# Casting q and k in the transfer, and turning them head by head

## The chip, the cores and the metric

The kernel runs on one core of one Trainium2 chip. The metric is the device time of one execution in microseconds (us). The kernel before took 433.94 us, the median of three runs (433.75 to 435.5).

## The reference

The inputs are q, k and v of shape (8 batches, 8 heads, 576 positions, 64), float32, eight global positions, and two weight matrices, 512 x 2048 and 2048 x 512. The attention is a local window of 32 positions to each side, with global rows and columns:

```python
scores = scale * np.matmul(q, k.transpose(0, 1, 3, 2))
mask = np.abs(pos[:, None] - pos[None, :]) <= window
mask = mask | is_global[:, None] | is_global[None, :]
scores = np.where(mask, scores, -1000000000.0)
attn = np.exp(scores - np.max(scores, axis=-1, keepdims=True))
attn = attn / (np.sum(attn, axis=-1, keepdims=True) + 1e-09)
attn_out = np.matmul(attn, v)
x = attn_out.transpose(0, 2, 1, 3).reshape(B * S, H * D)      # 4608 x 512
h = x @ w_in
g = np.maximum(h, 0.0) + np.log1p(np.exp(-np.abs(h)))         # softplus
out = g @ w_out                                               # 4608 x 512, float32
```

## The kernel before

The work is cut twice. Attention is cut into 72 units: a unit is one block of 64 positions of one batch, all eight heads, nine units to a batch. The two dense layers are cut into nine tiles of 512 tokens, that is eight units each, so a tile's borders and a batch's borders don't fall together. The matmuls of the dense layers are bf16, as are the matmuls of attention; scores and exponentials are float32.

For each batch there is a preparation. SP's queue loads k and q in float32 into three staging buffers `qk`, 72 partitions by 4 heads by 512 numbers (`load_qk`: each partition holds eight neighbouring positions of every head). Each half is two DMAs, of 64 and of 8 partitions. A cast (`add_cast`, L444 and L442) rounds it to bf16 and reorders it into `qn` or `kn`, one buffer each, so that the two heads of a pair stand side by side in 128 columns. TensorE transposes these (`tk`, `tq`, L512 and L518): eight transposes of 72 x 128 for each of the four head pairs, of k and of q. The results go to `kx` and `qz` by copies on ACT or DVE (`kev`, `qev`, L402). `pick` (L472) gathers the rows of the global positions out of `qn` and `kn` by 64 small matmuls. v is loaded in five pieces by SP (`load_v`, 256 bytes at a time), cast to `vA`, and a copy of it that is shifted by 64 rows, `vB`, is made by two DMAs from SBUF to SBUF (`shift`, L452 and L453).

A unit then runs as a chain over the engines: scores `s` on TensorE (L625), mask and row maximum on DVE (L631), exponentials `pe` on ACT (L652), row sums `sm` and reciprocals `rs` on DVE (L660 to L662), scaling to `pn` on POOL (L668), and the global columns `gw`, also POOL (L672), a transpose `tp` on TensorE (L678) and its copy `pt`. After four units `rt` (L704) and `xo` (L721, L728) make the attention output, and a copy of it is `xT`, the input of the dense layers. In batch 0 the first eight units take their row sums from ACT.

A tile runs its 64 matmuls `h` (L763), each 16th of them followed by a softplus `g` on ACT (L768), and then its 64 matmuls `o` (L773). The scores of the next tile's units lie among the `h` matmuls, and the exponentials, scaling and transposes among the `o` matmuls. A table load on ACT (L565) marks the step from softplus to the exponentials in each tile.

Each engine works through its queue in order. The order is made when the program is built: every piece of work is a job with a cost per engine, the jobs it depends on, a rank, and the buffers and PSUM banks that it opens or uses. `_Order.run` plays these jobs against a clock and takes, at each step, the one that could start first. A job of kind "DMA" is put on SP's queue; the weights are loaded by POOL's queue, which rounds them to bf16 on the way (`weights_in`, `weights_out`, L803 and L807, four DMAs each). The costs only decide the order and, where a job may run on several engines, which one takes it.

At the start SP loads k, q and v of batch 0. The casts of batch 0 are spread over DVE, ACT and POOL:

```python
            add_cast(b, 1, [["DVE"], ["ACT"], ["DVE"], ["DVE"]])
            add_cast(b, 0, [["DVE"], ["ACT"], ["POOL"], ["DVE"]])
            T["w_in"] = o.add({"POOL": (2400, 18000)}, weights_in, [T["cast", 0, 0][2]], rank=0)
            T["w_out"] = o.add({"POOL": (3000, 30000)}, weights_out, [T["cast", 0, 0][2]], rank=1)
            add_cast(b, 2, [["POOL", "ACT"]] * NT5)
```

All later casts are POOL's. The loads of batch 1 wait for a tiny DMA (`hold`) that reads the last piece of w_in. `blank_q` and `blank_g` clear the buffers of batches 0 and 1 on POOL, `make_band`, `mask_left`, `mask_right`, `mask_global`, `make_places` and `ones_g` build masks and places on DVE.

Of the kernel before, what the change touches and what calls it, by code (L numbers as in the profile page):

```python
# [18 lines left out]
class _Order:  # L19
# [15 lines left out]
    def add(self, cost, emit, deps=(), rank=5, opens=(), uses=(), table=None):  # L35

        job = dict(cost=cost, emit=emit, deps=[d for d in deps if d is not None], rank=rank, opens=list(opens),
                   table=table, n=len(self.jobs), at=None, end=None)
        self.jobs.append(job)
        for pool, key in job["opens"]:  # L40
            self.users.setdefault(key, []).append(job)
        for key in uses:
            self.users.setdefault(key, []).append(job)
        return job
# [30 lines left out]
    def run(self, free):  # L75
# [11 lines left out]
        dma = 0  # L87
        while ready:
            best = None
            for j in ready:  # L90
                t0 = max([d["at"] if d["on"] in j["cost"] and d["on"] in ("PE", "DMA") else d["end"] + self.HOP
# [27 lines left out]
            if e == "DMA":  # L119
                dma = max(dma, t + 1500) + took  # L120
                j["at"], j["end"] = t, dma + 500
            else:
                j["at"], j["end"] = t, t + took
# [14 lines left out]
def kernel(  # L138
# [10 lines left out]
    nc = tc.nc  # L149
# [47 lines left out]
    stage = ctx.enter_context(tc.tile_pool(name="stage", bufs=3))  # L197
# [9 lines left out]
    def load_qk(b, which, half):  # L207

        st = PS["in", b, which, half] = stage.tile([P, HP, QR * D], FP32, tag="qk", name="qk")
        src = SRC[which][b, half * HP:(half + 1) * HP].rearrange("h (q r) d -> q h (r d)", r=QR)  # L210
        for lo, hi in ((0, 64), (64, NQ)):
            nc.sync.dma_start(out=st[lo:hi, :, :], in_=src[lo:hi])

    qn = const([P, QR, H * D], BF16, "qn")
    kn = const([P, QR, H * D], BF16, "kn")
# [44 lines left out]

    mask = const([P, NJ, EXT], BF16, "mask")
# [29 lines left out]
    def mask_left():  # L291
        nc.vector.tensor_copy(mask[:, :, 0:G], band[:, 0:G].unsqueeze(1).to_broadcast([P, NJ, G]))
        nc.vector.memset(mask[:, 0, 0:WIN], NEG)

    def mask_right():
        nc.vector.tensor_copy(mask[:, :, W:EXT], band[:, G:P].unsqueeze(1).to_broadcast([P, NJ, G]))
        nc.vector.memset(mask[:, NJ - 1, EXT - WIN:EXT], NEG)
# [23 lines left out]
    def blank_q(i):  # L321
        for p in range(HP):
            nc.gpsimd.memset(qz[i][0:D, p, :, 1, :].bitcast(I32), 0)
            nc.gpsimd.memset(qz[i][D:P, p, :, 0, :].bitcast(I32), 0)

    def blank_g(i):
        nc.gpsimd.memset(kx[i][:, :, 0, 0:WIN].bitcast(I32), 0)
        nc.gpsimd.memset(kx[i][:, :, NH5 - 1, G - WIN:G].bitcast(I32), 0)
        clear(nc.gpsimd, pg[i][:])
        clear(nc.gpsimd, qg[i][:])  # L330
        clear(nc.gpsimd, lg[i][:])
        clear(nc.gpsimd, gw[i][:])
        nc.gpsimd.memset(vA[i][0:WIN, 0, :].bitcast(I32), 0)
        nc.gpsimd.memset(vA[i][96:P, NT5 - 1, :].bitcast(I32), 0)
        clear(nc.gpsimd, oz[i][:])
# [29 lines left out]
    SLOTS = dict(xT=2, osb=2, st=7, pe=3, pn=4, pt=5, R=2, small=2, gk=2, in_qk=3, in_v=3)  # L365
# [42 lines left out]
    def add_load(b, which, deps):  # L408
        if which < 2:
            parts = [(1700, lambda e, x=x: load_qk(b, which, x)) for x in range(2)]  # L410
        else:
            parts = [(1160, lambda e, x=x: load_v(b, x)) for x in range(NT5)]
        T["load", b, which] = [o.add({"DMA": (100 if which == 2 else 700, took)}, emit, deps, rank=0,
                                     opens=[("in_v" if which == 2 else "in_qk", ("in", b, which, x))])
                               for x, (took, emit) in enumerate(parts)]

    def add_cast(b, which, engines):
        n_parts = len(engines)
        early = []
        if which < 2:  # L420
            early += [T.get(("t" + "qk"[which], b - 1, p)) for p in range(HP)]
            early += [T.get(("pick", b - 1, x)) for x in range(2)]
        else:
            early += [T.get(("val", n4)) for n4 in range(NU)
                      if any((n4 * 4 + u) // NJ == b - 2 for u in range(4))]
            early += [T.get(("ov", b - 2)), T.get(("shift", b - 2)), T["blank_g", min(b, 1)]]
        T["cast", b, which] = []
        for n, who in enumerate(engines):
            loads = T["load", b, which]

            def emit(e, n=n):
                if which < 2:
                    to = (qn, kn)[which][:, :, n * P:(n + 1) * P].rearrange("q r (h d) -> q r h d", h=2)
                    at = PS["in", b, which, n // 2][:, n % 2 * 2:n % 2 * 2 + 2, :]
                    at = at.rearrange("q h (r d) -> q r h d", r=QR)
                else:
                    to, at = vA[b % 2][:, n, :], PS["in", b, 2, n][:, :]
                rows = [slice(0, NQ)] if which < 2 else {0: [slice(32, 64), slice(64, P)],
                                                         NT5 - 1: [slice(0, 96)]}.get(n, [slice(0, P)])
                for r in rows:  # L440
                    if e == "ACT":
                        nc.scalar.copy(to[r], at[r])  # L442
                    else:
                        (nc.gpsimd if e == "POOL" else nc.vector).tensor_copy(to[r], at[r])  # L444
            w = QR * P if which < 2 else H * D
            cost = {"POOL": (110 + .862 * w, 110 + .862 * w), "ACT": act(w, False), "DVE": dve(w, False)}
            T["cast", b, which].append(o.add({e: cost[e] for e in who}, emit,
                                             [loads[n * len(loads) // n_parts]] + early, rank=6 if b else 0,
                                             uses=[("in", b, which, n * len(loads) // n_parts)]))
        if which == 2:  # L450
            def shift(e):
                nc.sync.dma_start(out=vB[b % 2][0:64, :, :], in_=vA[b % 2][64:P, 0:NT5 - 1, :])  # L452
                nc.sync.dma_start(out=vB[b % 2][64:P, :, :], in_=vA[b % 2][0:64, 1:NT5, :])  # L453
            T["shift", b] = o.add({"DMA": (100, 3000)}, shift, T["cast", b, 2] + early, rank=0)

    def add_prep(b, gate, rank):
# [4 lines left out]
        if b < 2:  # L461
            blanks = {x: [T["blank_" + x, b]] for x in "qg"}
        XN = (qn, kn)

        def pick(e, ws):
# [3 lines left out]
            for w in ws:  # L469
                for r in range(QR):  # L470
                    for p in range(HP):
                        nc.tensor.matmul(out=PS["pick", b][p * 32:(p + 1) * 32, w, 0:P], lhsT=pick_w[0:NQ, r, :],  # L472
                                         rhs=XN[w][0:NQ, r, p * P:(p + 1) * P], start=(r == 0), stop=(r == QR - 1))
# [20 lines left out]
        for n, ws in enumerate(steps):  # L494
            T["pick", b, n] = o.add({"PE": (460 * len(ws) + 190, 460 * len(ws) + 300)}, lambda e, ws=ws: pick(e, ws),
                                    [x for w in ws for x in T["cast", b, w]] + [T.get(("pick", b, n - 1))], rank=4,
# [11 lines left out]
        for p in range(HP):  # L508
            def tk(e, p=p):
                ps = PS["tk", b, p] = psum(("tk", b, p), [P, QR, NQ], BF16)  # L510
                for r in range(QR):
                    nc.tensor.transpose(out=ps[:, r, :], in_=kn[0:NQ, r, p * P:(p + 1) * P],  # L512
                                        identity=ident_b[0:NQ, 0:NQ])

            def tq(e, p=p):
                ps = PS["tq", b, p] = psum(("tq", b, p), [P, QR, NQ], BF16)
                for r in range(QR):
                    nc.tensor.transpose(out=ps[:, r, :], in_=qn[0:NQ, r, p * P:(p + 1) * P],  # L518
                                        identity=ident_b[0:NQ, 0:NQ])
# [13 lines left out]
            T["tk", b, p] = o.add(mm(QR, NQ), tk, [T["cast", b, 1][p], *gate], rank=rank, opens=[("tk", ("tk", b, p))])  # L533
            T["kev", b, p] = o.add({"ACT": (640, 740), "DVE": (870, 950)}, kev, [T["tk", b, p], *late, *blanks["g"]],
                                   rank=3, uses=[("tk", b, p)])
            T["tq", b, p] = o.add(mm(QR, NQ), tq, [T["cast", b, 0][p], *gate], rank=rank, opens=[("tq", ("tq", b, p))])
# [77 lines left out]
    def add_scores(n, gate, rank):  # L614
# [19 lines left out]
        for x in range(2):  # L634
# [5 lines left out]
            T["top", n, x] = o.add({"DVE": (440, 600)}, lambda e, x=x: top(e, x), [T["sc", n, x], *T["mask", 0]], rank=4,  # L640
# [172 lines left out]
    for w in (1, 0, 2):  # L813
        add_load(0, w, T["load", 0, 0] if w == 2 else [])
    T["band"] = setup(make_band, {"DVE": (1500, 1600)}, rank=2)
    T["mask", 0] = [setup(fn, {"DVE": (cost, cost + 100)}, [T["band"]], 2)
                 for fn, cost in ((mask_left, 850), (mask_right, 850), (mask_global, 1400))]
    T["places"] = setup(make_places, {"DVE": (1300, 1400)}, T["mask", 0], 3)
    T["select"] = setup(select_rows, {"DVE": (500, 600)}, [T["places"]], 3)
    for i in range(2):  # L820
        T["blank_q", i] = setup(lambda i=i: blank_q(i), pool(2750), [T["load", 0, 2][-1]] if i else [], 1 + 5 * i)
        T["blank_g", i] = setup(lambda i=i: blank_g(i), pool(2400), [T["blank_q", i]], 1 + 5 * i)

    def add_ones(i, after):
        T["ones_g", i] = setup(lambda i=i: ones_g(i), {"DVE": (1500, 1600)}, [T["blank_g", i], T["places"], T["select"], *after],
                               1 + 5 * i)
# [12 lines left out]
    def make_batch(b, gate, rank):  # L839
# [3 lines left out]
        if b == 1:  # L843
            add_ones(1, [T["su", NJ - 3]])

            def hold(e):
                nc.sync.dma_start(out=held[0:1, :], in_=w_in_t[KD - 1][0:1, 0:16])
            T["hold"] = o.add({"DMA": (100, 100)}, hold, [T["w_in"], T["shift", 0]], rank=0)
        for w in (1, 0, 2):
            if b:  # L850
                add_load(b, w, [T["hold"]] if b == 1 else [T["cast", b - 1, w][-1]])
# [61 lines left out]
```

## Time and profile before

| what | value |
|---|---|
| median of three runs | 433.94 us (433.75 to 435.5) |
| the profiled execution | 437.42 us, of which the span of the profile is 435.7 |
| PE busy | 363.8 us, 83% of the span |
| PE weight loads | 203.3 us, 47% |
| ACT busy | 290.7 us, 67% |
| DVE busy | 257.0 us, 59% |
| POOL busy | 189.5 us, 44% |
| bytes moved by the DMA engines | 46.92 MB, of which 41.96 on SP's queue and 4.19 on POOL's |
| matmuls h, o | 134.8 and 135.1 us busy |

The profile is of one execution, and its times are counted from the start of its span. PE is TensorE's matmuls and PEld its weight loads, which overlap. "Busy" counts the time in which an instruction of the engine runs, and matmuls are pipelined, so that the busy time of one (0.2 us for a small one) is longer than the distance to the next. In a timeline, the time in brackets is the idle time of the engine before the row and what ended it. Idle time of an engine counts only where others wait for it. The DMA share is the mean busy share of 16 DMA engines, and goes over 1 where packets overlap. The trace also has a record of each DMA packet: its start, its queue and its size as written.

### The profile page before, as it was taken

How to read it: one execution, taken by the hardware profiler on the slowest of the kernel's cores; microseconds unless marked ns; L12 is line 12 of the kernel's file. 1: busy time of each engine (PE TensorE's matmuls, PEld its weight loads, DVE VectorE, ACT ScalarE, POOL GpSimd, SP SyncE). 2: the span in 40 equal slices, each digit the busy share in tenths (PEclk: the TensorE clock that was granted, in tenths of full speed). 3: DMA queues.
4: the chain of work that ended last, by engine and by line, in shares of the span. 5: the costliest groups of instructions: out<-in, count | busy, mean ns of one | idle time of the engine just before them, and what ended most of it. 6: DMA issues, size and time to landing. Idle time of an engine off the chain costs nothing.

```text
span 435.7 us, 12000 instructions
## 1 busy us (share of the span) xinstructions
PE 363.8 (83%) x4583; PEld 203.3 (47%) x4640; DVE 257.0 (59%) x1104; ACT 290.7 (67%) x717; POOL 189.5 (44%) x301
## 2 busy tenths in 40 slices
PE   0540769998999898998999899889988997998996
PEld 0420645555444644464446444645464444544442
DVE  3592746497539843695579447944894495547001
ACT  2471746887568863887588758876887785696730
POOL 6435786459215741376138513780461062036000
PEclk9999969999999998999999999999999999999999
DMA  7899999982961397129812881083114011002001
GB/s 153 136 207 225 220 163 177 181 175 84 220 126 48 99 190 140 48 70 197 162 48 71 199 159 50 26 170 69 50 46 98 0 50 52 0 24 74 3 24 72
DMA packets 56873, 46.92 MB, mean 108 GB/s; under 512 B 39408, under 2 KB 41456, under 8 KB 56816
## 3 DMA queue, kind: packets, MB, share of 16 engines
q1 hardware_dynamic: 54128, 41.96, 45.4%
q0 software_dynamic: 2688, 4.19, 5.3%
q8 instruction: 36, 0.59, 0.6%
q14 instruction: 21, 0.17, 0.1%
HBM read 36.71 MB, written 9.44 MB: 106 GB/s over the span
## 4 chain that ended last, share of the span: by engine, by line
PE 34%; DVE 21%; POOL 14%; DMA 13%; ACT 8%; issue 7%; SPq 2%; DVEq 0%; POOLq 0%; ACTq 0%
PE h L763 20%; DMA qk<-in_q_dram 7%; DVE sm L660 6%; PE o L773 6%; DMA v<-in_v_dram 5%; POOL kn L444 4%; POOL pn L668 3%; POOL qn L444 3%; DVE rs L662 3%; POOL vA L444 2%; DVE oz L596 2%; ACT L565 2%; DVE rs L661 2%; PE s L625 2%; DVE pt L402 2%
## 5 line engine op out<-in xcount | busy, mean ns | idle before, releaser
L763 PE MATMUL h<-xT,win 128*128 128x512 bf16 x552 | 134.8, 383 | 10.9 <-ACT xT L402 6.5
L668 POOL TENSOR_TENSOR pn<-pe,rs 128x512 bf16<-128x512 f32 x72 | 74.8, 1039 | 146.6 <-DVE rs L662 140.9
L773 PE MATMUL o<-wout,g 128*128 128x512 bf16 x543 | 135.1, 379 | 2.0 <-issue 0.8
L768 ACT ACTIVATE g<-h 128x512 bf16<-128x512 f32 x144 | 85.1, 597 | 58.4 <-PE h L763 58.2
L652 ACT ACTIVATE pe<-st,nb 128x136 f32<-128x136 f32 x288 | 94.3, 400 | 19.7 <-POOL gw L672 18.0
L631 DVE CUSTOM_DVE_ANT_0 st<-s,mask 128x136 f32<-128x136 f32 x288 | 69.7, 294 | 44.3 <-PE s L625 43.8
L763 PEld LDWEIGHTS <-win 128*128 128x128 bf16 x576 | 54.3, 99 | 62.6 <-issue 12.3
L773 PEld LDWEIGHTS <-g 128*128 128x128 bf16 x576 | 52.5, 98 | 48.0
L660 DVE TENSOR_REDUCE sm<-pe 128x4 f32<-128x544 f32 x64 | 45.5, 711 | 5.2 <-ACT pe L652 5.0
L444 POOL CAST qn<-qk 72x1024 bf16<-72x1024 f32 x29 | 30.1, 1066 | 36.4 <-DMA qk<-in_q_dram 35.0
L678 PE MATMUL tp<-ident_b,pn 128*128 128x128 bf16 x288 | 29.7, 230 | 18.9 <-POOL pn L668 15.1
L444 POOL CAST vA<-v 128x512 bf16<-128x512 f32 (+3 forms) x45 | 27.0, 608 | 26.5 <-DMA v<-in_v_dram 25.1
L678 PEld LDWEIGHTS <-pn 128*128 128x128 bf16 x288 | 17.9, 101 | 42.1 <-POOL pn L668 40.9
L625 PE MATMUL s<-kx,qz 128*128 128x136 bf16 x288 | 32.3, 235 | 2.7 <-DVE qz L402 2.3
L625 PEld LDWEIGHTS <-qz 128*128 128x128 bf16 x288 | 23.1, 103 | 18.7 <-DVE qz L402 2.6
L402 DVE COPY qz<-tq 64x576 bf16<-64x576 bf16 x32 | 23.5, 748 | 12.5 <-PE tq L518 8.9
L444 POOL CAST kn<-qk 72x1024 bf16<-72x1024 f32 x28 | 28.3, 1036 | 0.9 <-PE pick L472 0.7
L402 DVE COPY pt<-tp 128x512 bf16<-128x512 bf16 x51 | 21.3, 419 | 9.7 <-PE tp L678 9.0
L402 ACT COPY qz<-tq 64x576 bf16<-64x576 bf16 x32 | 20.3, 636 | 8.2 <-DVE qz L402 7.5
L402 ACT COPY kx<-tk 128x32 bf16<-128x32 bf16 (+1 forms) x75 | 19.1, 330 | 7.8 <-PE tk L512 7.7
L512 PE MATMUL tk<-ident_b,kn 72*128 72x72 bf16 x256 | 14.9, 209 | 11.1 <-ACT kn L442 9.8
L402 DVE COPY osb<-o 128x512 f32<-128x512 f32 x12 | 8.2, 686 | 26.4 <-PE o L773 26.4
(126 smaller groups left out, 447.2 us busy)
## 6 DMA issues: line engine op xcount, KB each, us to landing
out_dram<-osb SPq DMA_DIRECT2D x36, 256.0 KB
qk<-in_k_dram SPq DMA_DIRECT2D x16, 512.0 KB
qk<-in_q_dram SPq DMA_DIRECT2D x16, 512.0 KB
v<-in_v_dram SPq DMA_DIRECT2D x24, 256.0 KB
vB<-vA SPq DMA_DIRECT2D x16, 256.0 KB
v<-in_v_dram SPq DMA_DIRECT2D x16, 192.0 KB
win<-in_moe_w_in_dram POOLq DMA_DIRECT2D x4, 512.0 KB, 9.0
wout<-in_moe_w_out_dram POOLq DMA_DIRECT2D x4, 512.0 KB, 19.4
```

The source lines that it names most:

```text
L402: (nc.scalar.copy if e == "ACT" else nc.vector.tensor_copy)(out, in_)
L444: (nc.gpsimd if e == "POOL" else nc.vector).tensor_copy(to[r], at[r])
L512: nc.tensor.transpose(out=ps[:, r, :], in_=kn[0:NQ, r, p * P:(p + 1) * P], identity=ident_b[0:NQ, 0:NQ])
L625: nc.tensor.matmul(out=ps[:, y, :], lhsT=qz[i][:, x * 2 + y, j, :, :], rhs=kf[:, x * 2 + y, j * W:j * W + EXT], start=True, stop=True)
L631: nc.vector.tensor_tensor_reduce(out=PS["st", n][:, p, :], in0=PS["s", n, x][:, y, :], in1=mask[:, j, :], scale=-SCALE, scalar=3.0e38, op0 ...
L652: nc.scalar.activation(out=pe[:, p, 0:EXT], in_=PS["st", n][:, p, :], func=AF.Exp, bias=PS["nb", n][:, p:p + 1], scale=-1.0, **({"accum_ou ...
L660: nc.vector.reduce_sum(out=sm[:], in_=PS["pe", n][:, :, 0:EXT], axis=AX)
L668: nc.gpsimd.tensor_tensor(out=pn[:].rearrange("c p (a s) -> c p a s", a=2), in0=wide[:, :, :, 0:G], in1=rs[:].unsqueeze(2).unsqueeze(3).to ...
L678: nc.tensor.transpose(out=ps[:, p, :], in_=PS["pn", n][:, p, :], identity=ident_b[:])
L763: nc.tensor.matmul(out=h[:, :], lhsT=w_in_t[kd][:, c * P:(c + 1) * P], rhs=PS["xT", m][:, kd, :], start=(kd == 0), stop=(kd == KD - 1))
L768: nc.scalar.activation(out=t[:, :], in_=PS["h", m, c][:, :], func=AF.Softplus)
L773: nc.tensor.matmul(out=PS["o", m, ns][:, :], lhsT=PS["g", m, kf][:, ns * P:(ns + 1) * P], rhs=w_out_t[kf // 4][:, kf % 4, :], start=(kf == ...
```

## The change

q and k are loaded by POOL's queue, one DMA of 72 partitions for all eight heads, which rounds to bf16 on the way. The staging buffers and the casts of q and k go away. `qn` and `kn` become two buffers each, one for even and one for odd batches, and hold the heads one after the other. The transposes therefore work on one head at a time: 16 of 72 x 64 for each head pair in place of 8 of 72 x 128, the even head into the upper 64 partitions of PSUM and the odd one into the lower. `pick` reads the same rows in the new layout.

At the start POOL issues k and q of batch 0 first, then w_in, then k and q of batch 1, then w_out. v of batch 0 waits for a tiny DMA that reads `qn` of batch 0, and v of batch 1 for one that reads w_in. v has five staging buffers in place of three. From batch 2 on all loads wait for the last cast of the batch before. `blank_q` clears batch 0's buffers on DVE, one side of the mask may be copied by ACT, and the planner has a clock for each DMA queue and other costs. In the built program POOL's queue has, ahead of the first `pn`, the issues of batch 1's k and q and of w_out and all blanks; among the first eight `pn` the five casts of batch 1's v (in six instructions); and in later tiles four of the five casts of v (in five instructions, before: three casts in four) ahead of the eighth `pn`, then the last cast, and the issues of the next k and q. SP's queue has, for each batch, the four output stores of the second half of a tile, the two shifts, and then the five loads of the next v. On PE `pick` stands after 24 matmuls `h` in tiles 1 to 4 (before: after 40 or more).

```diff
-    def load_qk(b, which, half):
-        st = PS["in", b, which, half] = stage.tile([P, HP, QR * D], FP32, tag="qk", name="qk")
-        src = SRC[which][b, half * HP:(half + 1) * HP].rearrange("h (q r) d -> q h (r d)", r=QR)
-        for lo, hi in ((0, 64), (64, NQ)):
-            nc.sync.dma_start(out=st[lo:hi, :, :], in_=src[lo:hi])
-    qn = const([P, QR, H * D], BF16, "qn")
-    kn = const([P, QR, H * D], BF16, "kn")
+    qn = [const([P, H, QR * D], BF16, f"qn{i}") for i in range(2)]
+    kn = [const([P, H, QR * D], BF16, f"kn{i}") for i in range(2)]
+    def load_qk(b, which):
+        nc.gpsimd.dma_start(out=(qn, kn)[which][b % 2][0:NQ, :, :],
+                            in_=SRC[which][b].rearrange("h (q r) d -> q h (r d)", r=QR))
+    for which in (1, 0):
+        load_qk(0, which)
...
+    def blank_q(i, eng):
...
+    blank_q(0, nc.vector)
...
+    def mask_side(e, x):
+        copy(e, mask[:, :, x * W:x * W + G], band[:, x * G:x * G + G].unsqueeze(1).to_broadcast([P, NJ, G]))
...
-                                         rhs=XN[w][0:NQ, r, p * P:(p + 1) * P], start=(r == 0), stop=(r == QR - 1))
+                                         rhs=XN[w][0:NQ, p * 2:p * 2 + 2, r * D:(r + 1) * D],
+                                         start=(r == 0), stop=(r == QR - 1))
...
-                    nc.tensor.transpose(out=ps[:, r, :], in_=kn[0:NQ, r, p * P:(p + 1) * P],
-                                        identity=ident_b[0:NQ, 0:NQ])
+                    for h in range(2):
+                        nc.tensor.transpose(out=ps[h * D:(h + 1) * D, r, :],
+                                            in_=kn[i][0:NQ, p * 2 + h, r * D:(r + 1) * D],
+                                            identity=ident_b[0:NQ, 0:NQ])
...
+    for w in (1, 0):
+        add_load(0, w, [])
+    add_load(0, 2, [hold("v", T["load", 0, 0], qn[0][0:1, 0, 0:16])])
+
+    T["w_in"] = o.add({"POOL": (2400, 0)}, weights_in, [], rank=0, moves=("POOL", 14000))
+    for w in (1, 0):
+        add_load(1, w, [T["w_in"]])
+    T["w_out"] = o.add({"POOL": (3000, 0)}, weights_out, T["load", 1, 0], rank=1, moves=("POOL", 12000))
...
-            T["hold"] = o.add({"DMA": (100, 100)}, hold, [T["w_in"], T["shift", 0]], rank=0)
...
+            add_load(b, 2, [hold("w", [T["w_in"]], w_in_t[KD - 1][0:1, 0:16])])
+        elif b:
             for w in (1, 0, 2):
-                add_cast(b, w, [["POOL"]] * (HP if w < 2 else NT5))
+                add_load(b, w, [T["w_out"], T["cast", b - 1, 2][-1]])
+        add_cast(b, ["POOL"] if b else ["POOL", "ACT"])
```

## The prediction

> **What bounds the kernel now.** I read the page first (busy shares, the chain), then busy time by stretch, then the timelines of POOL, SP and PE. The page:
>
> ```profile
> span 435.7 us, 12000 instructions
> PE 363.8 (83%) x4583; PEld 203.3 (47%) x4640; DVE 257.0 (59%) x1104; ACT 290.7 (67%) x717; POOL 189.5 (44%) x301
> PE   0540769998999898998999899889988997998996
> DMA  7899999982961397129812881083114011002001
> ```
>
> TensorE bounds it, but the first five or six slices are thin on PE and full on DMA. By stretch (us, then busy us and count for PE, PEld, DVE, ACT, POOL; clock, DMA share, GB/s):
>
> ```profile
> 30.00:40.00 10.00, 1.91 (x28) 1.06 (x26) 4.34 (x28) 4.44 (x24) 2.54 (x7) 1.00 1.15 214
> 40.00:50.00 10.00, 4.25 (x35) 3.43 (x36) 6.05 (x44) 5.55 (x29) 8.00 (x20) 1.00 1.17 242
> 128.20:151.80 23.60, 21.35 (x367) 12.61 (x369) 19.48 (x56) 20.07 (x59) 13.47 (x22) 1.00 0.22 66
> 195.00:217.60 22.60, 20.05 (x269) 11.19 (x270) 12.31 (x71) 15.01 (x26) 9.09 (x10) 1.00 0.87 178
> ```
>
> So there are two regimes: a start short of data, then tiles of some 43 us, over 90% PE. The start, in POOL's timeline (start us, us, engine and line, what; in brackets the idle time before and what ended it):
>
> ```profile
> 20.36 2.35 POOL L803 DMA_DIRECT2D win<-in_moe_w_in_dram  x4
> 22.67 3.02 POOL L807 DMA_DIRECT2D wout<-in_moe_w_out_dram  x4
> 37.27 0.61 POOL L444 CAST vA<-v 96x512 bf16<-96x512 f32 x1 [11.58 <-DMA v<-in_v_dram]
> 43.18 1.04 POOL L668 TENSOR_TENSOR pn<-pe,rs 128x512 bf16<-128x512 f32 x1
> 57.78 1.04 POOL L668 TENSOR_TENSOR pn<-pe,rs 128x512 bf16<-128x512 f32 x1 [1.45 <-ACT kx L402]
> ```
>
> POOL issues the weights at 20.36, stands 11.58 us behind the last piece of v, blanks batch 1's buffers, and only at 43.18 scales the first unit; the eighth, which tile 0's w_in matmuls need, at 57.78. In a settled tile, rows of the timelines of POOL, SP and PE:
>
> ```profile
> 193.61 1.03 POOL L668 TENSOR_TENSOR pn<-pe,rs 128x512 bf16<-128x512 f32 x1
> 197.23 0.51 SPq L452 DMA_DIRECT2D vB<-vA  x1
> 199.92 0.40 PE L625 MATMUL s<-kx,qz 128*128 128x136 bf16 x4
> 210.92 0.61 PE L472 MATMUL pick<-qn,pick 72*32 72x128 bf16 x29 [0.36 <-POOL qn L444]
> ```
>
> The gather of global rows (pick) is the only place where PE waits for q: 2.9 us over all later tiles. What pick gathers here was issued by SP as the staging buffers came free, part of it a tile earlier, and cast by POOL.
>
> **Rates from the packet records.** Software queue alone: 203 packets/us of 1 KB written (w_out), 49/us of 4 KB (w_in). When SP's queue has work too, the two alternate one to one: 49 and 50/us at 28-33 us (w_in with v), about 150 and 150 at 34-36 (w_out with v's 256 B), 67 and 62 at 42-43 (w_out with vB's 4 KB). v alone: 400 to 980/us. First packet 2.55 us after an issue (20.36 to 22.9); a reader starts 0.75 us after the last.
>
> **The start, part by part.** k and q are 576 packets each: issued near 0.8, first packet 3.4, both moved by 9-10 and ready by 11, against 17.2 before. The casts vanish. w_in follows in the same queue: 512/49 = 10.5 us, to 20. v waits for q (the hold), starts near 13, and gets 49/us until w_in is through: 350 of 4608 packets. Its second piece, for which POOL's queue waits, lands near 24, its last at 28-29; ACT's queue holds casts of v ahead of the exponentials, so the first of these stays near 32 (29.65 before). POOL then issues k, q of batch 1 and w_out (4.5 us by L803/L807's 0.6-0.75 each), blanks batch 1's buffers (5.4 us by 37.81 to 43.18): first pn near 35, 8 us earlier. That is not kept; what is late next is batch 1's v. k and q run to 35, w_out's 2048 packets at 150/us to 49, and v gets the same 150/us: its pieces land near 39, 46, 51, 52 and 53. POOL's new order has their casts between pn 4 and pn 8, so the eighth pn comes near 54.5, not 57.78: 3.3 us gained. A further 1.0 us of batch-1 transposes leaves the w_in phase. Start: -4.3 us (-9 if v is not held back, 0 if SP issues v 4 us later). The other edits of the setup (DVE blanks batch 0's q and k buffers, ACT copies one side of the mask, the order of masks and ones) are 3 us of DVE and under 1 us of ACT at a time when both stand waiting for q and then v, until 28; I cost them at nothing, and at 3 us if v were early.
>
> **Turning by head.** 8 transposes of 128 columns become 16 of 64. Eight start every 0.26 us (191.62, 191.88, 192.14): 72 columns, 32.5 ns each. Bounds for 16: 0.26 us if two column tiles overlap fully, as four 32-column tiles do (xo L728: four 64-column matmuls per 29 ns); 0.52 us if they don't. Loads may pace them between. I take 0.4, as column tiles do overlap here: 8 x 0.14 = 1.1 us a batch, against 0.3 us of PE slack ahead of the eighth tp. The Trainium skill (TensorEngine Tiling (Array Packing), Restrictions) says that column tiling disables the fast weight load. With the P/1.2 ns that its page TensorE: Matmul & The Clock Gate, LDWEIGHTS (loading the stationary operand), gives a plain load of P columns, an estimate by these pages is 53 ns for each of two tiles side by side, 0.43 us for 16, and 1.4 us a batch where I take 1.1; no run here shows a 64-column load.
>
> **Settled tiles.** POOL loses 8 casts of 1.03 us, all off the path but for pick. One more v cast (0.58) now stands before the eighth pn: 193.61 becomes 194.2. Then gw, the last v cast, and only now the issue of the next k (196.0): the loads no longer run a tile ahead of their cast, so pick waits on the transfer itself. First packet 198.5. SP, released by the same cast, has vB's 128 packets of 4 KB (198.1 to 200.5), then v: k gets 125 packets by 200.5, the rest at 150/us ends at 203.5, q at 207.4, ready at 208.1. PE's new order puts pick after 24 w_in matmuls: 199.92 + 5.04 = 204.96, plus 0.6 to 1.2 of the above. So PE waits 2 to 2.5 us each tile. Behind pick on PE stand 40 w_in matmuls, for which ACT's softplus and then the next softmax wait, so nothing hides it: the tile is 208.1 - 204.96 = 3.1 us longer than with q in time (turning's cost is inside it). Alone on the engines, 1152/203 = 5.7 us, q would be ready at 205.0: no wait.
>
> The skill (DMA: Bandwidth & Descriptors, Why a DMA increments its semaphore by 16 and not by 1) has a rule against the new shape: a DMA spreads over the largest number of engines up to 16 that divides its slowest dimension, which for 72 rows is 12. By it, an estimate, the 9 us of k and q would stretch by up to a third, pick would wait 2.5 us more in five tiles, and the sum would be 451; its exception (some copies from the software queue still spread over all) would leave the sum below. The trace has no 72-row transfer, only SP's 64 and 8 rows.
>
> **Sum.** Periods between exp table loads before (82.50, 128.24, 174.45, 217.63, 260.79, 303.46, 344.85): 45.7, 46.2, 43.2, 43.2, 42.7, 41.4. New for the first four: 43.18 - 0.36 + 3.1 = 45.9, that is +0.2, -0.3, +2.7, +2.7. The fifth has pick later: +1.5; the sixth only the turning: +0.6. Together +7.4. After 1.5 us of pick waits at 165-167 the clock fell to half for 3.4 us (0.92 over 151.8-174.5); I allow one such fall, +1.7 (half of 3.4; that of before is already out of the second period). Total -4.3 + 7.4 + 1.7 = +4.8. The profiled run took 437.42 (span 435.7 plus 1.7 around it), 3.5 over the median of 433.94; added to the run it is 442.2, to the median 438.7, which is the forecast.
>
> **Rivals.** *q and k land before pick* (other side): the first packet is earlier or v yields the engines. It decides when issue to landing is under 10 us (196.0 to 205.9). For it: the 5.7 us alone. Against: the one-to-one rows. Then tiles 1 and 2 lose their old extra (45.7 and 46.2 to 43.6: -4.7), four pay 0.5 for cast and turning (+2), and the start gives -4.3: -7, 427. With batch 1's v unhindered too: 423.
> *Loss without limit in one place*: transposes serial (8 x 0.26 = 2.1 us a tile, partly under the wait) and clock halved in three more tiles: 438.7 + 5 + 2 = 446.
> *Cancelling*: waits of 1 us only: 434.
>
> **How the numbers follow.** Forecast case 0.44 (its own range 434.5 to 443), q in time 0.34, cancelling 0.12, serial 0.10. About 0.5% (2.2 us) is what a measurement tells from no change. Faster: 0.34 and a little of the cancelling case, 0.37; same 0.15; slower 0.48. Range 423 to 447.
>
> **What would show it.** Right: first pn near 35 and eighth near 54; pick waiting 2 us on DMA of q in tiles 1 to 4; 16 transposes in 0.3-0.5 us. Wrong: a k or q transfer under 10 us from issue, or an eighth pn before 50: then faster.

## The result, and the profile after

The changed kernel took 477.0 us (median of four runs, 474.59 to 477.57), the kernel before beside it 434.72 us: a ratio of 1.0945, 95% interval 1.087 to 1.1021. The forecast was 438.7 us with a range of 423 to 447, so the time is 30 us above the range. The profiled run took 477.57 us, its span is 475.9 us, 40.2 us longer than the span before.

The page of the changed kernel:

```profile
span 475.9 us, 12908 instructions
...
PE 384.9 (81%) x5152; PEld 212.1 (45%) x5152; DVE 256.4 (54%) x1109; ACT 290.1 (61%) x716; POOL 141.4 (30%) x249
...
PEclk9999679999699979998799979999799999999999
...
L458 PE MATMUL pick<-qn,pick 72*32 72x128 bf16 x256 | 7.5, 288 | 35.1 <-DMA qn<-in_q_dram 35.1
...
kn<-in_k_dram POOLq DMA_DIRECT2D x8, 576.0 KB, 11.6
qn<-in_q_dram POOLq DMA_DIRECT2D x8, 576.0 KB, 14.8
```

POOL lost 48 us of work (189.5 to 141.4) with the casts of q and k. But PE now stands 35.1 us in front of one instruction, `pick`, and the thing that ends the wait is the transfer of q itself. The clock row has a dip to 6 or 7 about every four slices of 11.9 us, once in each of five tiles, beside the one at the start. One settled tile, by the timelines of POOL, SP and PE (start us, us, engine and line, what, in brackets the idle time before and what ended it):

```profile
103.82 0.88 POOL L213 DMA_DIRECT2D kn<-in_k_dram  x1
104.70 0.80 POOL L213 DMA_DIRECT2D qn<-in_q_dram  x1
...
104.71 0.47 SPq L438 DMA_DIRECT2D vB<-vA  x1
105.27 0.55 SPq L439 DMA_DIRECT2D vB<-vA  x1
105.87 16.08 SPq L205 DMA_DIRECT2D v<-in_v_dram  x5
...
111.90 1.03 PE L754 MATMUL h<-xT,win 128*128 128x512 bf16 x4
121.39 1.04 PE L458 MATMUL pick<-qn,pick 72*32 72x128 bf16 x32 [8.46 <-DMA qn<-in_q_dram]
122.22 1.07 PE L458 MATMUL pick<-kn,pick 72*32 72x128 bf16 x32
123.22 1.89 PE L754 MATMUL h<-xT,win 128*128 128x512 bf16 x4
```

k and q leave POOL at 103.8 and 104.7, just as SP gives out vB and v. PE reaches `pick` at 112.9 and gets q at 121.4. After the wait, four `h` matmuls take 1.89 us; four ran in 1.03 before it. The same tile by stretches (stretch, us, then busy us and count for PE, PEld, DVE, ACT, POOL; granted clock, DMA share, GB/s):

```profile
107.00:123.00 16.00, 7.54 (x100) 4.41 (x98) 2.90 (x24) 5.02 (x8) 0.00 (x0) 0.81 0.99 165
...
123.00:128.00 5.00, 5.00 (x30) 2.17 (x22) 1.82 (x11) 1.57 (x3) 0.00 (x0) 0.58 0.16 37
```

PE works 7.5 of 16 us, and when it may go on it does so at little more than half clock. The table puts the five tiles together. The periods are those between exp table loads (82.20, 136.18, 187.82, 241.94, 293.66, 343.49, 385.01 after). The stretches of half clock are from the trace's record of the granted clock.

| tile | period after, before (us) | forecast of the difference | measured | wait of pick for q | half clock that began in the wait |
|---|---|---|---|---|---|
| 1 | 53.98, 45.74 | +0.2 | +8.2 | 8.46 | 10.24 |
| 2 | 51.64, 46.21 | -0.3 | +5.4 | 6.69 | 6.83 |
| 3 | 54.12, 43.18 | +2.7 | +10.9 | 8.62 | 10.24 |
| 4 | 51.72, 43.16 | +2.7 | +8.6 | 6.79 | 6.83 |
| 5 | 49.83, 42.67 | +1.5 | +7.2 | 4.32 | 6.83 |
| 6 | 41.52, 41.39 | +0.6 | +0.1 | none | none |

The start gave 0.3 us (82.20 against 82.50) where 4.3 were forecast, and what follows the last table load is equal (90.9 us in both). So the whole loss lies in five tiles, and it looks like 34.9 us of waits and the half clock behind them. Each fall of the clock begins inside its wait; 5.8, 4.9, 5.9, 4.9 and 5.6 us of half clock, 27.2 in all, lie behind the waits. The experiments had to show three things: that these waits are the cause and not the work, why the transfer takes so long, and where the forecast gain at the start went.

### The profile page after: what moved, and what is told of

Its sections match the earlier page's. It is cut to its first block, busy times and chain, and to the rows that moved or that the text cites. A ratio compares the mean times of both kernels' runs of the same rounds, so it can differ in the third digit from the quotient of the medians.

```text
span 475.9 us, 12908 instructions
## 1 busy us (share of the span) xinstructions
PE 384.9 (81%) x5152; PEld 212.1 (45%) x5152; DVE 256.4 (54%) x1109; ACT 290.1 (61%) x716; POOL 141.4 (30%) x249
## 4 chain that ended last, share of the span: by engine, by line
PE 41%; DMA 21%; DVE 18%; POOL 8%; ACT 6%; issue 5%; SPq 0%; POOLq 0%; DVEq 0%
PE h L754 22%; DMA qn<-in_q_dram 19%; PE o L764 8%; POOL pn L659 5%; DVE sm L651 5%; PE tp L669 3%; PE s L616 2%; DMA v<-in_v_dram 2%; DVE oz L587 2%; PE pick L458 2%; DVE rs L653 2%; POOL vA L431 2%; DVE st L622 2%; ACT L556 2%; DVE rs L652 1%
## 5 line engine op out<-in xcount | busy, mean ns | idle before, releaser
L754 PE MATMUL h<-xT,win 128*128 128x512 bf16 x576 | 145.0, 395 | 4.6 <-DVE xT L404 2.9
L764 PE MATMUL o<-wout,g 128*128 128x512 bf16 x576 | 140.6, 379 | 0.0
L669 PE MATMUL tp<-ident_b,pn 128*128 128x128 bf16 x288 | 29.9, 229 | 16.5 <-POOL pn L659 16.2
L458 PE MATMUL pick<-qn,pick 72*32 72x128 bf16 x256 | 7.5, 288 | 35.1 <-DMA qn<-in_q_dram 35.1
L616 PE MATMUL s<-kx,qz 128*128 128x136 bf16 x288 | 33.9, 243 | 1.4 <-DVE qz L404 0.8
L616 PEld LDWEIGHTS <-qz 128*128 128x128 bf16 x288 | 24.8, 108 | 19.9 <-issue 4.5
L458 PEld LDWEIGHTS <-pick 72*32 72x32 bf16 x512 | 11.8, 132 | 47.0 <-DMA qn<-in_q_dram 37.4
L404 DVE COPY qz<-tq 64x576 bf16<-64x576 bf16 x34 | 25.4, 751 | 6.7 <-PE tq L508 3.5
L404 DVE CAST gk<-pick 128x256 bf16<-128x256 f32 x6 | 2.5, 424 | 43.8 <-PE pick L458 43.7
L712 PE MATMUL xo<-R,oz 128*32 128x256 bf16 (+3 forms) x384 | 19.5, 258 | 5.5 <-ACT R L404 5.1
L622 DVE DVE_READ_ACCUMULATOR2_ANT nb<- 128x1 f32 x288 | 23.9, 83 | 0.0
## 6 DMA issues: line engine op xcount, KB each, us to landing
qn<-in_q_dram POOLq DMA_DIRECT2D x8, 576.0 KB, 14.8
```

What stands on the lines that cost most here:

```text
L404: (nc.scalar.copy if e == "ACT" else nc.vector.tensor_copy)(out, in_)
L616: nc.tensor.matmul(out=ps[:, y, :], lhsT=qz[i][:, x * 2 + y, j, :, :], rhs=kf[:, x * 2 + y, j * W:j * W + EXT], start=True, stop=True)
L622: nc.vector.tensor_tensor_reduce(out=PS["st", n][:, p, :], in0=PS["s", n, x][:, y, :], in1=mask[:, j, :], scale=-SCALE, scalar=3.0e38, op0 ...
L669: nc.tensor.transpose(out=ps[:, p, :], in_=PS["pn", n][:, p, :], identity=ident_b[:])
L754: nc.tensor.matmul(out=h[:, :], lhsT=w_in_t[kd][:, c * P:(c + 1) * P], rhs=PS["xT", m][:, kd, :], start=(kd == 0), stop=(kd == KD - 1))
L764: nc.tensor.matmul(out=PS["o", m, ns][:, :], lhsT=PS["g", m, kf][:, ns * P:(ns + 1) * P], rhs=w_out_t[kf // 4][:, kf % 4, :], start=(kf == ...
```

## Experiments: is it the wait?

**Loads a tile earlier.** The double buffers allow k and q of a batch to be issued long before the last cast of v of the batch before.

```diff
-                add_load(b, w, [T["w_out"], T["cast", b - 1, 2][-1]])
+                add_load(b, w, [T["w_out"], T["cast", b - (1 if w == 2 or b == 2 else 2), 2][-1]])
```

> The changed kernel, with k and q of batches 3 to 7 issued one tile earlier (they no longer wait for the last cast of v of the batch before; the double buffers allow it). Theory A, the transfer is late for pick: in the changed kernel k's issue to pick took some 17.5 us and pick waited 35 us in all, so with a tile more to land the waits of the later tiles go, the stretches of half clock that follow them go too, the exp periods fall from 50 to 54 back to 43 to 44 us, and the span comes to 432 to 441 us. Theory B, the loss sits in the work itself (64-column turning, a clock that falls for another reason): the span stays above 462.

Measured: 465.84 us, ratio 1.0749 (1.0713 to 1.0785), span 464.4. A miss for theory A as it was put; the span lies where theory B had it, above 462. The timelines of POOL and PE say why:

```profile
103.62 0.88 POOL L213 DMA_DIRECT2D kn<-in_k_dram  x1 [0.52 <-PE tk L500]
...
117.92 1.05 PE L458 MATMUL pick<-qn,pick 72*32 72x128 bf16 x32 [4.72 <-DMA qn<-in_q_dram]
...
154.65 0.88 POOL L213 DMA_DIRECT2D kn<-in_k_dram  x1
...
172.12 1.04 PE L458 MATMUL pick<-qn,pick 72*32 72x128 bf16 x32 [8.38 <-DMA qn<-in_q_dram]
```

The load did go one tile earlier, but the planner puts `pick` where it believes the load to be through, and it moved `pick` of the same batch one tile earlier too. The distance stayed at 14.3 and 17.5 us (103.62 to 117.92, 154.65 to 172.12), and so did the waits; there are four of them now, not five, 27.8 us in all. Since `pick` moved too, this run does not decide between the two theories, but it points at the planner's belief: it prices a transfer of k or q at 3.3 us.

**The same loads, pick planned later.** One number is changed, the planner's price of these transfers.

```diff
-                                     lambda e: load_qk(b, which) if b else None, deps + early, rank=5, moves=("POOL", 3300))]
+                                     lambda e: load_qk(b, which) if b else None, deps + early, rank=5, moves=("POOL", 8000 if b > 1 else 3300))]
```

> The changed kernel, with the planner told that a transfer of k or q of batches 2 to 7 takes 8 us of its queue instead of 3.3. Nothing moves on the queues; pick goes behind the w_in matmuls, 20 to 40 matmuls later on PE. Theory A: PE has 9 to 15 us of other work while the transfer runs, the waits for q fall under 2 us a tile, the clock stays full, and the span is 436 to 450. Rival: what stands behind pick (the rows of q and k, scores of the next batch, w_out's matmuls) becomes late instead, and the span stays above 455.

Measured: 430.64 us (ten runs), ratio 0.9924 (0.9888 to 0.9959): the span, 429.4, is below theory A's 436 to 450, and the kernel is faster than the one before by under 1%. POOL and SP issue the same transfers (a few casts of v changed places with `pn`). PE's timeline and the stretch from 107 to 123:

```profile
121.17 0.63 PE L458 MATMUL pick<-qn,pick 72*32 72x128 bf16 x32
```

```profile
107.00:123.00 16.00, 16.00 (x160) 8.18 (x158) 7.40 (x55) 10.69 (x19) 0.00 (x0) 1.00 0.92 162
```

`pick` has no bracket: nothing waits, PE is busy all 16 us at full clock, and 32 matmuls of `pick` take 0.63 us, not 1.04. No batch from 2 on waits for q. The rival, that what stands behind `pick` becomes late and keeps the span above 455, falls.

**Loads early, pick kept in its place.** This is the first experiment as it was meant: the early issue, and `pick` of batch b held behind 24 `h` matmuls of tile b-2. PE's order is that of the changed kernel except in tile 5, where `pick` stands after 24 `h` and not after 44.

```diff
-                add_load(b, w, [T["w_out"], T["cast", b - 1, 2][-1]])
+                add_load(b, w, [T["w_out"], T["cast", b - (1 if w == 2 or b == 2 else 2), 2][-1]])
...
-                                    [T["load", b, w][0] for w in ws] + [T.get(("pick", b, n - 1))], rank=4,
+                                    [T["load", b, w][0] for w in ws] + [T.get(("pick", b, n - 1)), T.get(("first", b - 2, 5))], rank=4,
```

> The early issue of k and q of the first experiment, with pick held where the changed kernel has it on PE (pick of batch b not before the 24th w_in matmul of tile b-2); PE's order is then that of the changed kernel. In the first experiment the planner had moved pick along with the loads, so the loads were early and the waits stayed. Theory A (the landing behind pick's place): no wait for q from tile 1 on, no stretch of half clock above 3.4 us there; by the waits taken away (34.9 us) and the half clock after them (some 13 us) the span is 428 to 435. Theory B (the loss is in the work or in the clock by itself): the span stays above 445.

Measured: 430.29 us, ratio 0.9891 (0.9834 to 0.9949); span of the profiled run 432.6, which is the longest of its four runs. PE's timeline and the same stretch:

```profile
112.07 0.63 PE L458 MATMUL pick<-qn,pick 72*32 72x128 bf16 x32
...
154.61 0.63 PE L458 MATMUL pick<-qn,pick 72*32 72x128 bf16 x32
```

```profile
107.00:123.00 16.00, 15.90 (x160) 8.35 (x161) 8.75 (x63) 9.73 (x17) 0.00 (x0) 1.00 0.94 172
```

Same work, the same order on PE, `pick` at 112.07 where the changed kernel reached it at 112.9, DMA share and GB/s about the same, and no wait. Theory A is shown. It also gives the price of the clock: the medians differ by 46.7 us (477.0 and 430.29), the waits were 34.9, so some 11.8 us are left for the half clock behind them. The 27.2 us of half clock there bound it from above: 13.6 us, if all the work in them took twice its time. In this profiled run one tile has a stall of 2.8 us at `pick` that the profile puts down to issue, with 3.4 us of half clock after it; its period is 47.3 and the others are 42.5 to 42.8. What it was stays open.

## Experiments: why does the transfer take so long?

In the packet records each transfer of k or q of the changed kernel ends with 12 packets of 4 bytes, each transfer of w_out with 16. The 1 KB packets take 96 ns each (median), as those of w_out do (96 to 98). If 72 rows run on 12 engines, 1152 packets are 96 an engine, 9.2 us back to back. On 16 they are 72, or 6.9 us.

**64 and 8 rows.**

```diff
-        nc.gpsimd.dma_start(out=(qn, kn)[which][b % 2][0:NQ, :, :],
-                            in_=SRC[which][b].rearrange("h (q r) d -> q h (r d)", r=QR))
+        src = SRC[which][b].rearrange("h (q r) d -> q h (r d)", r=QR)
+        for lo, hi in ((0, 64), (64, NQ)):
+            nc.gpsimd.dma_start(out=(qn, kn)[which][b % 2][lo:hi, :, :], in_=src[lo:hi])
```

> The changed kernel, with each transfer of k and q split into rows 0 to 63 and 64 to 71. In the changed kernel each of these transfers ends with 12 packets of 4 bytes where a transfer of w_out ends with 16, and the 1 KB packets take 96 ns each, 125 per us at most. Theory A1, 72 rows run on 12 DMA engines: with 64 rows on 16 the rate rises towards 167 per us, k and q land 3 to 5 us sooner (12.5 to 14.5 us from k's issue instead of 17.5), the waits shrink as much and the span comes to 448 to 460. Theory A2, the number of engines is not it, the sharing with vB and v on SP's queue is: landing within 1.5 us of 17.5, span 470 or more (two more issues on POOL are 1.6 us a batch).

Measured: 458.37 us, ratio 1.0599 (1.0526 to 1.0673), span 457.5. POOL's and PE's timelines:

```profile
100.91 1.31 POOL L215 DMA_DIRECT2D kn<-in_k_dram  x2
102.22 1.25 POOL L215 DMA_DIRECT2D qn<-in_q_dram  x2
...
115.41 1.04 PE L459 MATMUL pick<-qn,pick 72*32 72x128 bf16 x32 [5.41 <-DMA qn<-in_q_dram]
...
165.00 1.04 PE L459 MATMUL pick<-qn,pick 72*32 72x128 bf16 x32 [4.56 <-DMA qn<-in_q_dram]
```

From k's issue to `pick` it takes 14.5 us in tile 1 (before the split 17.6) and 13.7 in tile 2 (15.8). Over the five tiles the saving is 2.1 to 3.6 us, 2.8 in the mean. Each packet still takes 96 ns, but more of them start in one us: at most 189 in the settled tiles, where 72 rows had at most 154. Twelve sixteenths of the 203 that w_out reaches alone are 152. The saving is about what 72 for 96 packets an engine gives (2.3, an estimate from the 96 ns). The five waits fall from 34.9 to 21.2 us. Theory A1 fits all of this; the records don't name the engine of a packet, so the number twelve is read from counts and rates. The Trainium skill (DMA: Bandwidth & Descriptors, Why a DMA increments its semaphore by 16 and not by 1) says that a transfer uses the largest number of engines up to 16 that divides its slowest dimension, 12 for 72 rows, but that some copies of the software queue use all 16. By these counts the transfers here follow the rule and not the exception.

**v held until q has landed.**

```diff
-            for w in (1, 0, 2):
+            for w in (1, 0):
                 add_load(b, w, [T["w_out"], T["cast", b - 1, 2][-1]])
+            add_load(b, 2, [hold(("v", b), [T["load", b, 0][0], T["cast", b - 1, 2][-1]], qn[b % 2][0:1, 0, 0:16])])
```

> The changed kernel, with v of batches 2 to 7 issued only when q of the same batch has landed (PE's order is unchanged). Theory A1 (12 engines, 96 ns a packet): v's 256-byte packets take 20 to 30 ns each between them, so only 1 to 2 us a tile come back, the landing stays above 15.5 us and the span is 464 to 472. Theory A2 (sharing with v): the last 400 packets of q run at over 120 per us instead of 40 to 80, landing at 13 to 14.5 us, span 452 to 462.

Measured: 470.2 us, ratio 1.0844 (1.0801 to 1.0887), span 466.8. PE's timeline:

```profile
120.20 1.04 PE L458 MATMUL pick<-qn,pick 72*32 72x128 bf16 x32 [7.43 <-DMA qn<-in_q_dram]
...
170.91 0.94 PE L458 MATMUL pick<-qn,pick 72*32 72x128 bf16 x32 [4.97 <-DMA qn<-in_q_dram]
```

The landing is 16.5 and 14.1 us after k's issue, 1.0 and 1.7 us sooner; over the five tiles it is 1.0 to 2.5 us, 1.7 in the mean. So v's sharing is real and the smaller part; the span is A1's, the second landing is below what A1 said. The packet records show what neither theory had: with no other traffic left from 115 us on, q's packets in tile 1, from 113.5 us on, start at 123, 110, 102, 75, 42, 21 and 4 per us, at 98 ns each. 102 per us at 98 ns keep 10 engines busy, and then fewer and fewer: the engines are not done together. vB's 128 packets of 4 KB (268 ns each in the changed kernel, 2.1 us an engine) went over the same engines at the beginning; whether they make this tail was not separated.

## Experiment: what does the turning cost?

```diff
-                    nc.tensor.transpose(out=ps[:, r, :], in_=kn[0:NQ, r, p * P:(p + 1) * P],
-                                        identity=ident_b[0:NQ, 0:NQ])
+                    for h in range(2):
+                        nc.tensor.transpose(out=ps[h * D:(h + 1) * D, r, :],
+                                            in_=kn[0:NQ, r, p * P + h * D:p * P + (h + 1) * D],
+                                            identity=ident_b[0:NQ, 0:NQ])
```

(and the same for q, in the kernel before)

> The kernel before, with the turning alone changed: 16 transposes of 64 columns for each pair of heads in place of 8 of 128, from the same cast buffers. The prediction has 0.4 us for 16 (1.1 us more a batch, at most 8.8 in all, partly hidden): 435 to 442 us. If two column tiles run beside each other in full, 0.26 us and no change: 433 to 435. If they run one after the other and nothing hides it, 16 us: 445 to 450. The exp periods of the changed kernel's last tile (41.5 us against 41.4) speak for the first or second.

Measured: 437.41 us (twelve runs), ratio 1.0039 (1.001 to 1.0068), that is 0.4 to 3.0 us. PE's timeline, then the group of the weight loads (count, busy us, mean ns):

```profile
191.56 0.43 PE L521 MATMUL tq<-ident_b,qn 72*64 72x72 bf16 x16
191.81 0.43 PE L513 MATMUL tk<-ident_b,kn 72*64 72x72 bf16 x16
192.07 0.43 PE L521 MATMUL tq<-ident_b,qn 72*64 72x72 bf16 x16
```

```profile
L513 PEld LDWEIGHTS <-kn 72*64 72x64 bf16 x512 | 11.9, 121 | 16.4 <-ACT kn L442 9.8 <-issue 3.9 <-POOL kn L444 1.9
```

Sixteen start every 0.25 us, as eight of 128 columns did before (0.26). The 512 loads of 64 columns are busy for 11.9 us in all and last 121 ns each, so several are under way at a time. Why the kernel is still a trace slower (0.39%) isn't shown; the planner's order changed little.

## Experiments: where did the start's gain go?

In the changed kernel POOL's timeline has, ahead of the eighth unit:

```profile
50.34 0.61 POOL L431 CAST vA<-v 128x512 bf16<-128x512 f32 x1 [2.40 <-DMA v<-in_v_dram]
...
54.96 0.61 POOL L431 CAST vA<-v 128x512 bf16<-128x512 f32 x1 [2.82 <-DMA v<-in_v_dram]
...
58.75 1.06 POOL L659 TENSOR_TENSOR pn<-pe,rs 128x512 bf16<-128x512 f32 x1
```

**Both edits together:** the price of 8 us and the split of 64 and 8 rows, in the changed kernel.

```diff
+        for lo, hi in ((0, 64), (64, NQ)):
+            nc.gpsimd.dma_start(out=(qn, kn)[which][b % 2][lo:hi, :, :], in_=src[lo:hi])
...
+                                     lambda e: load_qk(b, which) if b else None, deps + early, rank=5, moves=("POOL", 8000 if b > 1 else 3300))]
```

> The changed kernel with both edits that helped: pick planned for a transfer of 8 us, and rows 0 to 63 and 64 to 71 as two transfers. With the rows split, the first exp table load of tile 0 came at 79.3 instead of 82.2 us, since q landed 2.3 us sooner at the start and the eighth scaled unit came at 56.5 instead of 58.8; in the later tiles there is no wait left to shorten. Theory A1: that start is kept, 427 to 429.5 us. Rival: two more issues on POOL a batch (1.6 us) stand before the scaling of units and take it back, 430 to 434.

Measured: 426.74 us, ratio 0.9792 (0.9751 to 0.9833). The first exp table load comes at 77.45, against 80.63 with the late pick alone; in the changed kernel the split alone moved it from 82.20 to 79.27. So the split's gain at the start, some 3 us, is kept.

**w_out behind batch 1's casts,** added to that:

```diff
+        if b == 1:
+            T["w_out"]["deps"].extend(T["cast", 1, 2])
```

> The kernel of both edits, with w_out issued behind the casts of batch 1's v instead of ahead of its blanks. The prediction had the eighth scaled unit at 54.5; the changed kernel had it at 58.8, behind two waits of POOL for v of 2.4 and 2.8 us, while w_out's 2048 packets shared the engines with v. If that sharing is what cost the predicted start, v's waits on POOL go, the eighth unit comes at 52 to 54 and the time is 423 to 427. If the exponentials set the pace (units 2.66 us apart before v is wanted), the eighth unit stays above 55 and the time within 1 us of the kernel of both edits. If w_out is then late for its first matmuls near 81 us, it is slower.

Measured: 428.81 us, ratio 0.9846 (0.9801 to 0.989): not faster than without this edit, and above the 423 to 427 of its theory. **And w_out behind the eighth unit too:**

```diff
+    T["w_out"]["deps"].append(T["no", 7])
```

> The kernel of the run before (rows split, late pick, w_out behind the casts of batch 1's v), with w_out also behind the eighth scaled unit. In the run before POOL's waits for v were gone and the casts went by 50.2 to 51.3, but the four issues of w_out (3.08 us) then stood before the eighth unit at 54.35. Theory, the start is bound by POOL's eighth unit: it comes at 51.3 and the first exp table load of tile 0 some 3 us sooner than 79.0, 424 to 426 us. Rival, something else of the start is bound (tile 0's scores, ACT's exponentials, PE's rows of batch 1): the table load stays within 1 us of 78 to 79 and the time at 426 to 430; if w_out lands after 80 us, its first matmuls wait and it is slower than that.

Measured: 425.68 us, ratio 0.9746 (0.9706 to 0.9787). POOL's timeline, of the run with w_out behind the casts, then of the one with w_out last:

```profile
51.29 3.08 POOL L799 DMA_DIRECT2D wout<-in_moe_w_out_dram  x4
54.35 1.09 POOL L660 TENSOR_TENSOR pn<-pe,rs 128x512 bf16<-128x512 f32 x1
```

```profile
52.67 1.04 POOL L660 TENSOR_TENSOR pn<-pe,rs 128x512 bf16<-128x512 f32 x1 [1.37 <-DVE rs L654]
53.85 3.08 POOL L799 DMA_DIRECT2D wout<-in_moe_w_out_dram  x4
```

With w_out out of the way POOL no longer waits for v at all, where with both edits it still stood 2.41 and 0.78 us (the casts are over at 51.3; with both edits at 54.7, in the changed kernel at 57.9). So the sharing with w_out was that delay. In the first of the two runs w_out's own issues took what was won; its table load is at 79.04. In the second it is at 74.59, 7.6 us ahead of the changed kernel, and the eighth unit now waits for its reciprocals on DVE. This version beats both kernels; the interval of the one with both edits overlaps with its own.

**Early loads, pick kept, 64 and 8 rows:** the edit of the third experiment and the split, in the changed kernel.

```diff
+        for lo, hi in ((0, 64), (64, NQ)):
+            nc.gpsimd.dma_start(out=(qn, kn)[which][b % 2][lo:hi, :, :], in_=src[lo:hi])
...
+                                    [T["load", b, w][0] for w in ws] + [T.get(("pick", b, n - 1)), T.get(("first", b - 2, 5))], rank=4,
...
+                add_load(b, w, [T["w_out"], T["cast", b - (1 if w == 2 or b == 2 else 2), 2][-1]])
```

> The changed kernel's order on PE kept, k and q of batches 3 to 7 issued a tile early, and the rows split into 64 and 8. Theory: with the loads in time nothing of the 72 rows is left but the start, where the split brought some 3 us: 426 to 429 us, within 1.5 us of the kernel with the late pick and split rows. Rival: the extra issues on POOL cost as much as they bring: 430 or more.

Measured: 426.6 us, ratio 0.9779 (0.9742 to 0.9817), the same as the late pick with split rows, as expected: the two ways to cover the transfer are worth the same.

## Why the prediction was wrong

The mechanism was the forecast's own: PE stands at `pick` for the transfer of q. Its size was wrong. The six tiles were to cost 7.4 us and cost 40.4.

**Where pick stands: right.** The forecast let PE reach `pick` 9.0 us after k's issue (196.0 to 204.96). It was 9.1 in tiles 1 to 4 (103.82 to 112.93 in the first).

**When q lands: the step that failed.** The prediction said that k gets 125 packets in the first 2 us, "the rest at 150/us", q ready 12.1 us after k's issue. This landing is the term that was mis-sized. Measured were 17.6, 15.8, 17.7, 15.9 and 15.7, a mean of 16.5; in tile 1 the 1152 packets took 14.8 us, 78 per us. The rates were read from w_out's transfers, which have 128 rows, and applied to transfers of 72. The kernel before had lower ones too: from 44 to 50 us w_out's packets beside SP's of 2 KB start at 51 to 99 per us. The forecast landing is 4.4 us too early. The split won 2.8 in the mean (fewer engines for 72 rows) and holding v 1.7 (its sharing); no run has both, so that the two add up to the 4.4 is likely and not shown. The wait was thus 8.5 us in tile 1 where 3.1 more per tile were counted, and 4.3 in tile 5 where 1.5 were.

**The rule that was weighed and left out** of the sum, 12 engines for 72 rows, fits what was measured. By it the forecast would have been 451, which the prediction's text gave but its range and chances did not take in. The rule alone was not enough either. Of the other 26 us some 10 are the clock (11.8 for 1.7), 4.0 the start, and some 9 v's sharing (five tiles at 1.7); the rest isn't separated.

**The clock: mis-sized.** One fall of 3.4 us (1.7 us lost) was allowed. There were five, of 6.8 to 10.2 us, 41.0 in all and 27.2 of them behind the waits, and they cost some 11.8 us. Over all runs here with a wait of PE for q in a settled tile, the wait of 1.5 us had no fall behind it, one of 2.6 us had 3.4 us of half clock, and those of 4.3 us and more had 3.4 to 10.2, always a multiple of 3.41. A short idle time can be enough: in the kernel before the fall at 167.2 followed 3.41 us in which PE was idle for 1.5, and with the late pick one at 190.9 followed 3.41 us with 1.65 idle, without any wait for q; yet 1.72 us idle in the 3.41 from 150.1 on, in the kernel before, brought none. The Trainium skill (TensorE: Matmul & The Clock Gate, Part 1: The HAM clock gate) has a window of about 3.4 us without work after which the array drops to half its clock, and one of sustained work to come back. The step of 3.41 us agrees, and before each of the five falls here PE was idle for 3.1 to 3.4 us of 3.41; the falls after 1.5 and 1.65 us do not agree with a window without any work.

**The turning: too dear.** 0.4 us for 16 was taken, 0.25 us measured, 1.1 us a batch against 0.4 to 3.0 us for all eight. The estimate of 0.43 us from two pages of the Trainium skill (TensorEngine Tiling (Array Packing), Restrictions, and TensorE: Matmul & The Clock Gate, LDWEIGHTS (loading the stationary operand)) is refuted by the same rows: sixteen loads of 64 columns, into two halves of the array, and their transposes start every 0.25 us.

**The start: too early by 2.5 us at the first unit and by 4.3 at the eighth.** First `pn` at 37.48 (forecast 35), eighth at 58.75 (54.5). Two steps failed. One is again the rate of 72 rows: q of batch 0, forecast to be ready by 11, was read at 12.95, and the split alone brought the first `pn` to 36.25 and the first table load 2.9 us forward. The other is v's rate beside w_out: its second and third piece, forecast for 46 and 51, ended POOL's waits at 50.34 and 54.96, and these two waits are 5.2 us. The start gave 0.3 us for 4.3.

**The rivals.** "q and k land before pick" had 0.34 and a price of 427. As built the kernel went the other way. Where q was in time, with the same order on PE but in tile 5, it took 430.29; tiles 1 and 2 then lost their old extra, as that rival said (42.7 and 42.5 us, before 45.7 and 46.2). Its first exp table load came at 81.41, 1.1 us ahead of the kernel before where 4.3 were forecast: these are the 3 us that it lacks to 427. So the change is worth about 1% without the waits, and the waits with their half clock add some 11% (477.0 against 430.29).

## What to carry to other kernels

Price a transfer by its packets per engine, with the engines that its row count gives, and add what the other queues put on those engines in the same window; a rate read from a transfer of another shape is no bound. Where the order of an engine is made from estimated costs, a merged or moved transfer needs a new estimate: here one number, 3300 to 8000, was worth 46 us, and moving the load alone was worth 11, because its reader moved with it. The waits of TensorE cost about a third more than their own length here, through the clock (11.8 on 34.9 us).

## What was not expected of the hardware

A casting transfer of 72 rows begins with 196 packets of 4 bytes and ends with 12. A pair of 64 and 8 rows has 96 in all. At 9 ns each (median) the small packets cost little. What the first 196 are for isn't shown, but the counts fit twelve engines: 576 packets are 48 for each, and 196 is four engines with 48 small packets and a closing one; of the 96, 16 are the closing ones of the 64 rows, 8 those of the 8 rows, and eight idle engines with 8 small packets and a closing one make 72. And 64-column weight loads of two heads overlap so far that halving the tiles costs the transposes no time on PE (0.25 us for sixteen, 0.26 for eight).
